# A PE-bound recurrent-attention and wave-mixing kernel: clock-keeping matmuls moved ahead of the spread of w, and a new order table

## The chip, the cores and the metric

The kernel runs on one core of one Trainium2 chip. The metric is the device time of one execution in microseconds (us), median of the runs. The engines are named as in the profile: PE (TensorE, matmuls), PEld (its weight loads), DVE (VectorE), ACT (ScalarE), POOL (GpSimd) and SP (SyncE, which only issues DMAs here).

## The reference

Two layers follow each other, for a batch of 4, 768 steps and 8 heads of 48:

```
for t in range(S):                       # one state of 48x48 per head
    cur   = outer(u * k_t, v_t)
    y_t   = r_t @ (state + cur)
    state = w * state + outer(k_t, v_t)
x   = heads of y side by side            # (4, 768, 384)
th  = x @ w_theta
yy  = w_tok_r @ (x * cos(th)) + w_tok_i @ (x * sin(th))   # over the 768 steps
u   = x + yy
out = u + max(u @ w_ch, 0)
```

## The kernel before

The recurrence is turned into matmuls over chunks of 128 steps. Powers of w that depend on the step are multiplied into r and k (`rscale` L553, `kscale` L566), the scaled tiles are transposed on PE (L516) and evacuated by ACT (L275), scores are formed (L614) and masked on DVE (L619), and the output of a pair of chunks is the sum of a masked part (L717) and a part from the running state (L712). The state is built from outer products (L672). The step's own term with u goes through `PD` (L626, L632), L641, `dg` and `yd` (L648, POOL). So one pair of chunks gives a piece of x (L726); there are three pairs in a batch element. From x come theta (L743), sine and cosine (L747, L750), `zr` (L753, DVE) and `zi` (L756, POOL). The token weights are loaded in row tiles 0 to 5 of each matrix, cast to bf16 on ACT or POOL, transposed on PE (L500) and evacuated; then the mixing (L774, 288 matmuls of 384 columns), `un` (L782), the channel matmul (L799), `fin` (L804) and the store (L808) follow. Mixing of one batch element is interleaved with attention of the next.

The tiles of the token weights in this text: `ld_99` to `ld_104` hold row tiles 0 to 2 (r0, i0, r1, i1, r2, i2), `ld_89` to `ld_94` tiles 3 to 5 (r3, i3, r4, i4, r5, i5). So `ld_90` is i3 and `ld_91` is r4.

The order of all work is written out by hand. `build` registers 816 tasks; the table `ORDER` (L27) lists each task's number, its engine (0 PE, 1 DVE, 2 ACT, 3 POOL, 4 SP) and the PSUM tiles that it takes, and `follow` (L178) emits them in that order. Each engine works through its own tasks strictly in that order and waits where an input is not there. The costs that stand with each task, such as `(1000, 217)`, are notes for the search that made the table; the emitted program does not use them.

The start matters here. The row w is loaded by ACT's queue (task 0, L336), spread over the 128 partitions by one f32 matmul against a row of ones (task 17, L405), and ACT takes its logarithm (task 18, L408) and six exponentials (tasks 19 to 24, L414) whose scale is the step number `tok_f` (POOL iota, task 8, then a DVE cast, task 9). These give the tables `wpow` for r, and `wpinvj` (first batch element) and `wpinv` for k.

Two groups of matmuls compute nothing. Both multiply a tile of zeros by itself into a PSUM tile that nobody reads: `before_w` (task 16, L402) and 108 `warm` tasks of two matmuls each (tasks 32 to 139, L817, depending on `zeros` and on the spread of w). The table scatters the warm tasks over places in PE's order; 28 of them (56 matmuls) stand behind the last useful matmul. They are called fillers below.

All loads go through SP's queue in table order, into a ring of 19 buffers.

Of the kernel before, what the change touches and what calls it, by code (L numbers as in the profile page):

```python
# [20 lines left out]
PE, DVE, ACT, POOL, SP = "PE", "DVE", "ACT", "POOL", "SP"  # L21
# [6 lines left out]
    (0, 2), (3, 1), (10, 3), (2, 1), (4, 1), (1, 2), (146, 4), (8, 3), (11, 1), (13, 3), (6, 1),  # L28
    (7, 2), (9, 1), (5, 1), (144, 4), (17, 0, 0), (14, 3), (153, 3), (145, 4), (16, 0, 1), (18,
    2), (12, 3), (24, 2), (20, 2), (15, 3), (178, 4), (19, 2), (32, 0, 4), (22, 2), (33, 0), (147,  # L30
    1), (34, 0), (21, 2), (35, 0), (25, 0, 2), (23, 2), (179, 4), (36, 0), (37, 0), (26, 1), (148,
    0, 1), (150, 1), (27, 2), (38, 0), (39, 0), (40, 0), (149, 2), (41, 0), (42, 0), (181, 1),
    (43, 0), (180, 4), (151, 0, 0), (44, 0), (164, 0, 3), (152, 2), (30, 1), (45, 0), (182, 0, 5),
    (184, 1), (142, 4), (46, 0), (28, 2), (47, 0), (154, 0, 1), (31, 3), (156, 0, 0), (160, 1),
    (212, 4), (155, 2), (48, 0), (49, 0), (50, 0), (157, 1), (51, 0), (187, 3), (52, 0), (161, 0,
    2), (165, 2), (53, 0), (158, 0, 1), (54, 0), (162, 2), (183, 2), (140, 4), (55, 0), (163, 3),
    (159, 1), (56, 0), (185, 0, 2), (168, 0, 0), (143, 2), (166, 0), (248, 4), (186, 2), (57, 0),
    (169, 0), (215, 3), (167, 1), (58, 0), (59, 0), (60, 0), (170, 1), (213, 4), (29, 2), (61, 0),
    (62, 0), (192, 0, 1), (198, 0, 2), (193, 1), (171, 0, 3), (249, 3), (199, 2), (270, 4), (63,
    0), (216, 0, 5), (172, 1), (141, 2), (64, 0), (188, 0, 0), (194, 1), (190, 0, 1), (214, 4),  # L40
    (189, 2), (200, 0), (218, 1), (65, 0), (66, 0), (217, 2), (67, 0), (68, 0), (191, 1), (69, 0),
    (195, 0, 3), (173, 0, 0), (269, 4), (196, 2), (197, 3), (201, 1), (70, 0), (202, 0, 1), (174,
    2), (268, 4), (71, 0), (203, 0), (175, 2), (72, 0), (221, 3), (219, 0, 2), (204, 1), (73, 0),
    (74, 0), (75, 0), (220, 2), (276, 3), (76, 0), (256, 4), (77, 0), (78, 0), (176, 1), (250, 0,
    3), (205, 0, 5), (251, 2), (79, 0), (224, 0, 1), (244, 4), (222, 0, 0), (225, 1), (273, 3),
    (80, 0), (232, 0, 2), (223, 2), (260, 4), (277, 0, 3), (206, 1), (233, 2), (81, 0), (226, 0,
    0), (264, 4), (278, 2), (82, 0), (228, 1), (274, 0, 5), (207, 0, 1), (227, 1), (245, 3), (275,
    2), (252, 4), (257, 3), (83, 0), (84, 0), (229, 0, 2), (208, 2), (284, 1), (306, 4), (85, 0),
    (282, 0, 0), (265, 3), (86, 0), (230, 2), (209, 2), (87, 0), (283, 1), (246, 0, 3), (272, 4),
    (88, 0), (231, 3), (285, 0, 2), (247, 2), (89, 0), (90, 0), (91, 0), (92, 0), (210, 1), (266,  # L50
    0, 5), (286, 2), (261, 2), (330, 4), (280, 0, 0), (258, 0, 3), (307, 3), (281, 1), (267, 2),
    (234, 0, 1), (235, 0), (177, 3), (253, 2), (308, 0, 2), (271, 4), (236, 1), (262, 0, 5), (259,
    2), (93, 0), (94, 0), (254, 0, 0), (332, 4), (95, 0), (211, 3), (263, 2), (237, 0, 1), (255,
    1), (96, 0), (97, 0), (396, 0, 3), (238, 1), (309, 2), (403, 0, 5), (310, 4), (239, 0, 0),
    (279, 2), (335, 3), (322, 4), (397, 0), (240, 2), (404, 0), (288, 0, 2), (398, 0), (241, 2),
    (302, 4), (289, 1), (287, 3), (405, 0), (292, 0, 1), (290, 0), (406, 0), (242, 1), (314, 4),
    (98, 0), (293, 0), (243, 3), (399, 0), (294, 1), (407, 0), (331, 4), (415, 0, 0), (416, 0),
    (291, 1), (417, 0), (303, 3), (336, 0, 1), (364, 4), (418, 0), (323, 3), (337, 2), (400, 0),
    (419, 0), (420, 0), (338, 3), (315, 2), (318, 4), (401, 0), (421, 1), (99, 0), (408, 0), (311,
    2), (402, 1), (304, 0, 2), (334, 4), (295, 0, 0), (409, 1), (305, 2), (324, 0, 1), (339, 0,  # L60
    3), (325, 1), (296, 2), (333, 4), (410, 0, 5), (319, 3), (340, 1), (316, 0, 2), (411, 2),
    (297, 0, 1), (317, 1), (369, 3), (365, 4), (346, 1), (312, 0, 5), (298, 2), (342, 0, 0), (366,
    4), (313, 1), (100, 0), (422, 0, 3), (299, 2), (343, 1), (341, 3), (423, 0), (424, 0), (326,
    4), (347, 0, 2), (350, 0, 5), (300, 1), (348, 2), (344, 0, 0), (349, 3), (351, 2), (320, 0,
    2), (486, 4), (345, 1), (425, 0), (321, 2), (352, 0), (426, 0), (372, 3), (354, 0, 1), (353,
    1), (328, 4), (427, 0), (355, 0), (428, 1), (441, 0, 5), (368, 4), (356, 1), (442, 0), (370,
    0, 0), (301, 3), (373, 0, 3), (367, 4), (371, 2), (434, 0, 2), (374, 1), (357, 0, 1), (443,
    0), (491, 3), (454, 4), (380, 1), (358, 2), (101, 0), (378, 0, 0), (102, 0), (329, 2), (103,
    0), (379, 1), (429, 0, 3), (455, 4), (327, 2), (444, 0), (359, 0, 1), (375, 2), (430, 1),
    (487, 4), (376, 0, 0), (360, 2), (435, 0), (377, 1), (436, 0), (453, 4), (361, 2), (445, 0),  # L70
    (461, 3), (381, 0, 3), (437, 0), (382, 2), (362, 1), (412, 0, 0), (457, 4), (383, 3), (492, 0,
    3), (413, 1), (438, 0), (493, 2), (456, 4), (439, 0), (446, 0), (440, 1), (384, 0, 0), (458,
    3), (431, 0, 1), (447, 1), (414, 4), (385, 1), (448, 0, 5), (488, 4), (432, 1), (386, 0, 0),
    (464, 3), (449, 2), (104, 0), (387, 0), (459, 0, 3), (490, 4), (388, 1), (462, 0, 2), (460,
    2), (105, 0), (106, 0), (473, 0, 5), (463, 1), (389, 0, 1), (489, 4), (494, 3), (450, 0, 0),
    (474, 1), (390, 2), (469, 1), (519, 4), (475, 0), (391, 0, 1), (476, 1), (363, 3), (451, 1),
    (495, 0, 2), (392, 2), (520, 4), (569, 0, 3), (496, 1), (570, 0), (393, 2), (550, 0, 5), (395,
    3), (502, 1), (571, 0), (521, 4), (497, 2), (551, 0), (394, 1), (552, 0), (572, 0), (606, 4),
    (467, 0, 0), (524, 3), (465, 0, 1), (468, 1), (503, 0, 2), (573, 0), (638, 4), (504, 2), (574,
    0), (506, 0, 2), (466, 1), (527, 3), (553, 0), (507, 2), (554, 0), (555, 0), (523, 4), (470,  # L80
    0, 0), (508, 0), (556, 1), (500, 0, 1), (471, 2), (575, 1), (498, 0, 0), (505, 3), (525, 0,
    5), (607, 4), (509, 1), (107, 0), (528, 0, 3), (501, 1), (526, 2), (557, 0, 2), (522, 4),
    (472, 3), (558, 0), (529, 2), (559, 0), (499, 1), (576, 0, 5), (605, 4), (560, 0), (643, 3),
    (477, 0, 1), (561, 0), (535, 1), (478, 0), (510, 0, 0), (530, 2), (479, 1), (433, 4), (511,
    0), (562, 0), (587, 0, 3), (512, 1), (480, 4), (577, 0), (610, 3), (108, 0), (531, 0, 1),
    (563, 1), (533, 0, 0), (109, 0), (532, 1), (588, 0), (513, 4), (536, 0, 2), (578, 0), (579,
    0), (534, 1), (539, 0, 1), (580, 0), (540, 2), (589, 0), (608, 4), (537, 1), (581, 0), (538,
    3), (541, 0, 0), (582, 1), (481, 0, 1), (639, 4), (613, 3), (110, 0), (542, 0), (482, 2),
    (609, 4), (590, 0), (543, 1), (594, 0, 2), (483, 2), (564, 0, 5), (595, 0), (485, 3), (565,
    2), (544, 4), (596, 0), (484, 1), (514, 0, 0), (566, 0, 1), (671, 4), (515, 2), (516, 2),  # L90
    (597, 0), (518, 3), (567, 1), (591, 0), (614, 0, 5), (640, 4), (517, 1), (598, 0), (611, 0,
    1), (616, 3), (599, 0), (615, 1), (452, 4), (612, 2), (592, 0), (545, 0, 0), (600, 1), (583,
    4), (593, 1), (621, 1), (619, 0, 1), (546, 2), (644, 0, 3), (620, 1), (622, 0, 2), (547, 2),
    (601, 4), (549, 3), (709, 0, 5), (710, 0), (623, 2), (711, 0), (645, 2), (548, 1), (625, 0,
    1), (702, 0, 2), (703, 0), (676, 3), (642, 4), (626, 1), (704, 0), (712, 0), (627, 0), (584,
    0, 0), (568, 4), (628, 1), (646, 3), (713, 0), (641, 4), (585, 1), (617, 0, 1), (677, 0, 3),
    (618, 1), (705, 0), (672, 4), (678, 2), (706, 0), (624, 3), (707, 0), (714, 0), (673, 4),
    (647, 0, 3), (715, 1), (629, 0, 0), (602, 0, 1), (648, 2), (708, 1), (675, 4), (649, 2), (727,
# [144 lines left out]
def build(ctx, tc, nc, r, k, v, w, u, moe_w_theta, moe_w_tok_r, moe_w_tok_i, moe_w_ch, out):  # L243
# [12 lines left out]
    P = Plan(SLOTS)  # L256
# [77 lines left out]
    def setup():  # L334
# [40 lines left out]
        def pads(ts):  # L375
            for t in ts:
                nc.gpsimd.memset(t[:, :, :, D:], 0.0)
        P.add({POOL: (750, 100)}, lambda e: pads(Rws), wr=[("Rw", i) for i in range(2)],
              prio=-197)
# [489 lines left out]
```

## Time and profile before

| what | value |
|---|---|
| median of 5 runs | 141.47 us (140.96 to 142.12) |
| the profiled execution's own time | 141.85 us |
| its span, first to last instruction | 140.2 us |
| PE busy | 134.6 us (96%), 1669 matmuls, 216 of them fillers of L817 |
| DVE, ACT, POOL busy | 102.6, 71.6, 89.2 us |
| last useful matmul group starts | 133.75 us, ends 134.90 us |
| DMA | 27.59 MB, mean 197 GB/s |

A matmul's duration in this profile is its latency, not its cost: matmuls overlap, and a group of n that the profile shows as taking t has a spacing of (t minus one latency) / (n - 1). The PE row counts fillers as busy, so "96%" is not a share of useful work.

### The profile page before, as it was taken

How to read it: one execution, taken by the hardware profiler on the slowest of the kernel's cores; microseconds unless marked ns; L12 is line 12 of the kernel's file. 1: busy time of each engine (PE TensorE's matmuls, PEld its weight loads, DVE VectorE, ACT ScalarE, POOL GpSimd, SP SyncE). 2: the span in 40 equal slices, each digit the busy share in tenths (PEclk: the TensorE clock that was granted, in tenths of full speed). 3: DMA queues.
4: the chain of work that ended last, by engine and by line, in shares of the span. 5: the costliest groups of instructions: out<-in, count | busy, mean ns of one | idle time of the engine just before them, and what ended most of it. 6: DMA issues, size and time to landing. Idle time of an engine off the chain costs nothing.

```text
span 140.2 us, 4016 instructions
## 1 busy us (share of the span) xinstructions
PE 134.6 (96%) x1669; PEld 98.1 (70%) x1669; DVE 102.6 (73%) x147; ACT 71.6 (51%) x110; POOL 89.2 (64%) x81
## 2 busy tenths in 40 slices
PE   3799999999999999999999999999999999999993
PEld 1698888788678778578667766766775756565673
DVE  5266897898375998789989965897799968344650
ACT  3845998899819747727625217671620044400020
POOL 7805838997998889694999769659384245400000
PEclk9999999999999999999999999999999999999999
DMA  3999999898999899969999687989499280907451
GB/s 101 269 261 294 311 202 293 277 317 163 310 308 232 188 289 178 207 151 214 188 218 208 177 154 142 208 213 259 99 250 174 56 98 19 281 2 188 148 180 50
DMA packets 72445, 27.59 MB, mean 197 GB/s; under 512 B 67050, under 2 KB 70891, under 8 KB 72427
## 3 DMA queue, kind: packets, MB, share of 16 engines
q1 hardware_dynamic: 72400, 27.34, 84.8%
q8 instruction: 13, 0.21, 0.7%
q14 instruction: 6, 0.04, 0.1%
q10 hardware_dynamic: 26, 0.00, 0.0%
HBM read 20.06 MB, written 4.72 MB: 177 GB/s over the span
## 4 chain that ended last, share of the span: by engine, by line
PE 86%; DMA 9%; ACT 1%; POOL 1%; DVE 0%; ACTq 0%; issue 0%; DVEq 0%
PE bank L774 34%; PE bank L516 10%; PE bank L799 8%; PE bank L817 8%; PE bank L743 8%; DMA ld<-in_moe_w_tok_i_dram 6%; PE bank L614 4%; PE bank L672 3%; PE bank L717 3%; DMA wu<-in_u_dram 3%; PE bank L712 2%; PE bank L500 2%; PE bank L641 1%; PE bank L680 1%; PE bank L600 1%; POOL ld L277 1%
## 5 line engine op out<-in xcount | busy, mean ns | idle before, releaser
L774 PE MATMUL bank<-zi,WiT 128*128 128x384 bf16 x144 | 33.5, 326 | 0.0
L774 PE MATMUL bank<-zr,WrT 128*128 128x384 bf16 x144 | 33.2, 326 | 0.0
L619 DVE TENSOR_TENSOR mAT<-bank,mask 128x1024 bf16<-128x1024 f32 x24 | 28.9, 1218 | 3.1 <-PE bank L614 2.8
L756 POOL TENSOR_TENSOR zi<-x,sin 128x768 bf16<-128x768 bf16 x12 | 19.6, 1640 | 10.9 <-ACT sin L747 10.9
L648 POOL TENSOR_TENSOR yd<-dg,vb 128x768 bf16<-128x768 f32 x12 | 17.6, 1472 | 8.0 <-ACT dg L275 6.7
L817 PE MATMUL bank<-zeros 128*128 128x128 bf16 x216 | 20.8, 232 | 0.0
L569 POOL TENSOR_TENSOR Kw<-ld,wpinv 128x768 bf16<-128x768 f32 x9 | 16.3, 1814 | 5.9 <-DMA ld<-in_k_dram 5.9
L275 ACT ACTIVATE RT<-bank 128x1024 bf16<-128x1024 bf16 x12 | 12.3, 1023 | 13.7 <-PE bank L516 12.6
L553 POOL TENSOR_TENSOR Rw<-ld,wpow 128x768 bf16<-128x768 f32 x10 | 18.1, 1815 | 1.0 <-DMA ld<-in_r_dram 1.0
L774 PEld LDWEIGHTS <-WrT 128*128 128x128 bf16 x144 | 12.8, 98 | 6.8
L774 PEld LDWEIGHTS <-WiT 128*128 128x128 bf16 x144 | 12.8, 97 | 6.7
L747 ACT ACTIVATE sin<-bank 128x768 bf16<-128x768 f32 x12 | 9.7, 810 | 15.1 <-PE bank L743 13.2
L804 DVE SCALAR_TENSOR_TENSOR fin<-bank,un 128x768 f32<-128x768 f32 (+1 forms) x13 | 11.5, 894 | 7.4 <-PE bank L799 7.3
L782 DVE TENSOR_TENSOR un<-bank,x 128x384 bf16<-128x384 f32 x24 | 12.7, 553 | 5.7 <-PE bank L774 5.1
L817 PEld LDWEIGHTS <-zeros 128*128 128x128 bf16 x216 | 14.7, 103 | 2.4 <-issue 0.3
L799 PE MATMUL bank<-Wch,uT 128*128 128x384 bf16 x72 | 13.7, 326 | 0.3 <-ACT uT L275 0.3
L743 PE MATMUL bank<-Wth,xT 128*128 128x384 bf16 x72 | 13.7, 326 | 0.0
L726 DVE TENSOR_TENSOR x<-bank,yd 128x768 bf16<-128x768 f32 x12 | 11.4, 956 | 3.1 <-PE bank L717 1.9
L753 DVE TENSOR_TENSOR zr<-bank,x 128x768 bf16<-128x768 f32 x12 | 11.4, 952 | 2.8 <-ACT bank L750 2.6
L750 ACT ACTIVATE bank<-bank,pi 128x768 f32<-128x768 f32 x12 | 10.5, 873 | 0.0
L275 ACT ACTIVATE uT<-bank 128x768 bf16<-128x768 bf16 (+1 forms) x5 | 3.3, 681 | 13.5 <-PE bank L516 13.5
L799 PEld LDWEIGHTS <-uT 128*128 128x128 bf16 x72 | 6.7, 98 | 4.5 <-ACT uT L275 0.5
(95 smaller groups left out, 221.1 us busy)
## 6 DMA issues: line engine op xcount, KB each, us to landing
ld<-in_r_dram SPq DMA_DIRECT2D x12, 384.0 KB, 5.6
out_dram<-fin SPq DMA_DIRECT2D x11, 384.0 KB, 2.6
ld<-in_k_dram SPq DMA_DIRECT2D x18, 192.0 KB, 4.4
ld<-in_v_dram SPq DMA_DIRECT2D x18, 192.0 KB, 5.5
ld<-in_moe_w_tok_i_dram SPq DMA_DIRECT2D x6, 384.0 KB, 6.1
ld<-in_moe_w_tok_r_dram SPq DMA_DIRECT2D x6, 384.0 KB, 5.6
ld<-in_v_dram SPq DMA_DIRECT2D x3, 384.0 KB, 6.0
ld<-in_k_dram SPq DMA_DIRECT2D x3, 384.0 KB, 6.2
```

The source lines that it names most:

```text
L275: nc.scalar.activation(dst, src, Act.Copy)
L516: nc.tensor.matmul(bank16(tok)[:, i * C:(i + 1) * C], s, ident, is_transpose=True, start=(i == 0), stop=(i == n - 1))
L553: P.add(mul(g, 2.15), lambda e: eng_of[e].tensor_mul(Rw[:, :, :, :D].transpose([0, 2, 1, 3]), Ls[ir].rearrange("p (h n d) -> p h n d", h=H ...
L569: eng_of[e].tensor_mul(Kw[:, :, :, :D].rearrange("p a h d -> p (a h) d"), Ls[ik].rearrange("p (a d) -> p a d", d=D), wpinv.rearrange("p a ...
L619: P.add({DVE: dve_op(8 * C)}, lambda e, tk=tk, c=c: nc.vector.tensor_mul(mAT[:, c].rearrange("p a h t -> p (a h) t"), dbl(tk).rearrange("p ...
L648: P.add({POOL: pool_op(2 * HD, 1.7)}, lambda e: eng_of[e].tensor_mul(yd.rearrange("p a (h d) -> p (a h) d", h=H), wide(dg, D), vb.rearrang ...
L743: nc.tensor.matmul(dbl(th)[:, t, :HD], xT[:, ND * t + dk, :], Wth[:, dk, :], start=(dk == 0), stop=(dk == ND - 1))
L756: P.add({POOL: pool_op(2 * HD, 1.9)}, lambda e: eng_of[e].tensor_mul(zi[:, 2 * pr:2 * pr + 2], x[:, 2 * pr:2 * pr + 2], sn), rd=xk + [("si ...
L774: nc.tensor.matmul(bank(tm)[:, :HD], WT[:, so, to * C:(to + 1) * C], z[:, so], start=(so == 0 and part == 0), stop=(part == 2 * NP - 1 and ...
L782: P.add({DVE: dve_op(HD)}, lambda e, tm=tm, t=t, to=to: nc.vector.tensor_add(un[:, t], bank(tm)[:, :HD], x[:, to]), use=[tm], rd=[("x", zj ...
L799: nc.tensor.matmul(dbl(tf)[:, t - lo, :HD], uT[:, ND * t + dk, :], Wch[:, dk, :], start=(dk == 0), stop=(dk == ND - 1))
L817: nc.tensor.matmul(bank("warm")[:, :C], zeros, zeros, start=True, stop=True, skip_group_check=True)
```

## The change

The values in the table change, and three notes on costs with it; one count in the code changes, from 8 to 9 matmuls in `before_w`. No other function differs.

```diff
-        P.add({ACT: (550, 1600)}, small_loads, wr=["w_row"], prio=-200)
+        P.add({ACT: (550, 950)}, small_loads, wr=["w_row"], prio=-200)
...
-        P.add({ACT: (1370, 3400)}, wu_load, rd=["table"], wr=["wu"], prio=-198)
+        P.add({ACT: (1370, 2800)}, wu_load, rd=["table"], wr=["wu"], prio=-198)
...
-            for _ in range(8):
+            for _ in range(9):
                 nc.tensor.matmul(bank("pre")[:, :C], zeros, zeros, start=True, stop=True,
                                  skip_group_check=True)
-        P.add({PE: (1000, 217)}, before_w, rd=["zeros"], acq=[("pre", 1)], prio=-201, name="pre")
+        P.add({PE: (510, 217)}, before_w, rd=["zeros"], acq=[("pre", 1)], prio=-201, name="pre")
...
 ORDER = [
-    (0, 2), (3, 1), (10, 3), (2, 1), (4, 1), (1, 2), (146, 4), (8, 3), (11, 1), (13, 3), (6, 1),
-    (7, 2), (9, 1), (5, 1), (144, 4), (17, 0, 0), (14, 3), (153, 3), (145, 4), (16, 0, 1), (18,
+    (0, 2), (4, 1), (10, 3), (3, 1), (2, 1), (16, 0, 0), (1, 2), (144, 4), (14, 3), (11, 1), (17,
+    0, 3), (7, 2), (13, 3), (145, 4), (32, 0, 4), (8, 3), (33, 0), (18, 2), (34, 0), (12, 3), (9,
...
```

On PE the order at the start was: L405, 8 of L402, 8 fillers, the small transpose L419 (it waits for the load of u), 4 fillers, transposes of r. It is now: 9 of L402, L405, 40 fillers, transposes of k, 4 fillers, L419, transposes of r, 10 fillers and so on. Of the 216 fillers of L817, 12 stood ahead of the first transposes and 56 behind the last useful matmul; now it is 40 and 58. In between there are 148 before and 118 after, and of these 118 all but 6 now stand ahead of the first mixing matmul.

On the other engines: `zeros` is the first instruction of DVE, not the third. POOL builds `spread` (task 14) and clears the pads of k's tiles (task 13) ahead of the iota (task 8). The six exponentials run in the order wpinv, wpinvj, wpow, wpinvj, wpinv, wpow, where it was wpinvj, wpow, wpow, wpinv, wpinv, wpinvj. DVE scales k before r. The cast of v for the first batch element (L277 on POOL, three times) is done by ACT; POOL casts one more token tile, and ACT six more of the half-state copies (L694) that DVE did as three instructions (L690). The third `rscale` moves from POOL to DVE and the third `kscale` from DVE to POOL.

On SP's queue the loads come as r, k, v, k, r, r, theta (2 of 3 parts), v, k, theta (1 of 3), then r and k of the second batch element, v, and six token tiles with r0 first; it was v, r, k, r, k, v, theta (1 of 3), r, theta (2 of 3), i0, k, and so on. The tile i3 (`ld_90`) was the 21st load and is the 22nd, with one more half load of v ahead of it. Its transposes on PE stand right behind the first two mixing matmuls.

## Prediction

> **What bounds the kernel now.** I read the page's head first, then PE's timeline of the first 22 us, then the chain, then busy time by stretch.
>
> ```profile
> span 140.2 us, 4016 instructions
> PE 134.6 (96%) x1669; PEld 98.1 (70%) x1669; DVE 102.6 (73%) x147; ACT 71.6 (51%) x110; POOL 89.2 (64%) x81
> PEclk9999999999999999999999999999999999999999
> L817 PE MATMUL bank<-zeros 128*128 128x128 bf16 x216 | 20.8, 232 | 0.0
> ```
>
> PE carries the span, but 216 of its matmuls are fillers, so its 96% must be split into needed work, fillers and stalls. The clock row shows nothing at the start; the spacing of equal matmuls does:
>
> ```profile
> 2.22 1.61 PE L405 MATMUL bank<-w_row,ones 1*128 1x384 f32 x2 [2.22 <-DMA w_row<-in_w_dram]
> 3.77 1.03 PE L402 MATMUL bank<-zeros 128*128 128x128 bf16 x8
> 4.59 1.06 PE L817 MATMUL bank<-zeros 128*128 128x128 bf16 x8
> 6.46 0.24 PE L419 MATMUL bank<-ident_f,wu 8*128 8x8 f32 x1 [0.80 <-DMA wu<-in_u_dram]
> ...
> 7.18 1.01 PE L516 MATMUL bank<-ident,Rw 128*128 128x128 bf16 x8
> 7.99 1.49 PE L817 MATMUL bank<-zeros 128*128 128x128 bf16 x12
> 9.27 1.06 PE L516 MATMUL bank<-ident,Kw 128*128 128x128 bf16 x8
> ...
> 11.41 0.86 PE L516 MATMUL bank<-ident,Rw 128*128 128x128 bf16 x8
> ...
> 13.08 0.73 PE L817 MATMUL bank<-zeros 128*128 128x128 bf16 x10
> ```
>
> Twelve fillers from 7.99: (1.49 - 0.31) / 11 = 107 ns apart. Ten from 13.08: (0.73 - 0.22) / 9 = 56 ns. The group at 11.41 is mixed. So PE ran at half speed until about 11.9 us, 5.4 us after its last gap (5.65 to 6.46, waiting for u).
>
> Needed work at full speed, spacing by the same arithmetic: mixing, theta and channel 432 matmuls x 162.5 ns = 70.2; transposes 258 + 72 at 56 = 18.3; scores 192 x 34 = 6.6; L717 192 x 25 = 4.8; L712 80 x 43 = 3.4; L672 40 x 55 + 60 x 44 = 4.8; L641, L680, L600 together 4.9. Sum 113.1 us. From the first transposes (7.2) to the end of the last channel matmul (134.9) are 127.7 us: 113.1 needed, 148 fillers x 56 ns = 8.2, cold surcharge on some 18 of these fillers 0.9 and on 32 needed matmuls 1.35, and 4.1 left over as stalls. Fillers and stalls lie almost all before 35 us: after it only about 34 fillers (1.9 us) and some 1.6 us of stalls stand between 94 us of needed work. The kernel is a ramp in which PE lacks input, then PE alone.
>
> What feeds the ramp: loads that land 1.5 us apart (DVE's timeline; the bracket is its wait).
>
> ```profile
> 7.60 0.96 DVE L566 TENSOR_TENSOR Kw<-ld,wpinvj 128x768 bf16<-128x768 f32 x1 [0.49 <-DMA ld<-in_k_dram]
> 9.04 0.96 DVE L553 TENSOR_TENSOR Rw<-ld,wpow 128x768 bf16<-128x768 f32 x1 [0.48 <-DMA ld<-in_r_dram]
> 10.54 0.96 DVE L566 TENSOR_TENSOR Kw<-ld,wpinvj 128x768 bf16<-128x768 f32 x1 [0.30 <-DMA ld<-in_k_dram]
> ```
>
> From 20 to 35 us (columns: length, then PE, PEld, DVE, ACT, POOL, clock, DMA share, GB/s) ACT is busy 13.99 of 15:
>
> ```profile
> 20.00:35.00 15.00, 14.91 (x274) 12.62 (x272) 12.85 (x15) 13.99 (x22) 12.47 (x11) 1.00 0.94 255
> ```
>
> And the chain (start, length, what) runs through a landing:
>
> ```profile
> 23.83 8.67 DMA ld<-in_moe_w_tok_i_dram
> 32.56 0.83 POOL ld L277
> 33.44 0.84 PE bank L500 x12
> ```
>
> This is tile i3: 8.7 us from issue, landed at 32.5, cast on POOL, transposed on PE at 33.44.
>
> **The change, part by part.**
>
> *Early fillers and clock.* `zeros` becomes DVE's first fill (0.88, 0.17 long), so L402 can start near 1.2; nine at 107 ns end at 2.2, when w lands. L405 starts as before (2.22) and ends at 3.83, so the logarithm is where it was (3.87): cost nothing, covered by the wait for w. Then 40 fillers, without a gap. When does the clock rise? By the nearest row, 5.4 us after the last gap: 1.2 + 5.4 = 6.6. The Trainium skill ("TensorE: Matmul & The Clock Gate", Part 1) states a window of about 3.4 us that runs freely: from 4.6, and up to 8.0 if a window had just begun. By 4.6 the 40 fillers end at 6.5, by 6.6 at 7.4 (26 cold, 14 warm), by 8.0 at 8.1. I take 6.6. The same section speaks against the change: it puts the ramp's penalty at under 1% of a typical span (1.4 us here). The rows say: 1.35 on needed work and 0.9 on fillers ahead of it, 2.25 us.
>
> *First inputs.* The iota now stands behind `spread` and k's pads on POOL (0.33 + 1.12 + 1.10), so `tok_f` comes near 4.4; the first exponential was at 4.38: at most 0.2 lost. With six exponentials 0.47 apart, both wpinvj stand after the fourth (6.4), k lands second (5.98): k scaled by 7.35, fillers done at 7.4, so transposes start at 7.4 against 7.2. r follows: scaled 8.25, ACT casts v (7.55 to 8.3), evacuates k (9.3) and r (10.4). Both together were ready at 11.4, but scores started only at 12.8, because PE was 1.5 us behind, in cold fillers. They now start near 10.4. On DVE behind it: masks from 12.0 (13.27), x of pair 0 near 15.7 (16.7), of pair 1 near 20.4 (23.2). First sine near 20.2 (22.2). So the front of the ramp moves by 2 to 2.8 us.
>
> *PE's sum.* 7.4 + 113.1 + 118 fillers x 56 ns = 6.6 + stalls. With stalls as before (4.1) the end is 131.2: 3.7 us earlier.
>
> *Do the later inputs follow?* ACT gets three casts of v (0.85 each) and the half copies. From the first to the third sine it worked 15.1 us almost without idle; I count 15.1 again, so the third comes near 35.3 (37.3): 2.0 gained, not more. DMA gains nothing from the clock: i3 has one half load more ahead of it. At the cadence without a pause it would land at 30.7; before it should by that have landed at 29.9 and landed at 32.5, the pauses in SP's queue being 2.6 us. Bounds 30.7 and 33.3. Its transposes stand as PE's third item of the mixing, and PE is in order: what waits behind are the first zi parts and all mixing; behind its cast on POOL wait zi of pair 1, `yd`, `rscale`. With landing at 33.3 PE passes there at 34.2, where it stood at 34.1 before with the same needed work done; with 30.7 it passes 2.3 earlier. I take the middle, 32.2: about 1.0 gained there. The next late tile, r4, comes out the same (0 to 1.5). Behind that point before had 1.9 us of fillers left, and after has 0.1 before the final group; of these 1.8 I take 1.1, as some covered real waits. Gain 1.0 + 1.1 = 2.1.
>
> *Free edits.* The 58 final fillers (56) lie beside the last evacuation and store. The half copies take ACT 0.66 where DVE took 0.56, three times, on an engine idle for half of the time after 50 us. L419 now behind k's transposes: u landed at 6.4, nothing waits for it on PE.
>
> **Rivals.**
> - *Likeliest: the ramp's inputs hold it to part of the gain*, 2.1 us: 141.5 - 2.1 = 139.4. Chance 0.45, own range 138.3 to 140.6.
> - *Full gain*: DMA pauses shrink, stalls stay 4.1: 3.7 us, 137.8. For it: the front moves 2 to 2.8 us, and fillers in the middle vanish. Against: ACT at 93% and the landings. 0.20.
> - *No change*: i3 lands at 33.3, r4 after 44, and the fillers that vanish turn into stalls of the same length, since each stood where an input was awaited: within 0.7 of 141.5, say 141.2. 0.15. Here belongs too that the clock rises only near 8.
> - *Slower*: place, the transposes of i3 in PE's order, in front of ready mixing. PE has 1.9 us in hand there (fillers dropped behind it), so the loss begins when it passes after 36.0, that is when i3 lands after 35.1, 1.8 later than my late bound. Each us beyond is one us of the span. A pause of SP's queue like the 2.6 us before, once more, on top: 33.3 + 2.6 = 35.9, and the same again at r4 (0.6): 1.4 lost, 142.9. 0.20.
>
> **Numbers.** The sums are against the profiled execution (span 140.2; 141.85 with what lies around it), 0.4 above the median; I apply the difference to the median: 139.4. Faster by over 0.5% (0.7 us, about what a measurement of this kernel can tell from no change) 0.65, within 0.15, slower 0.20. Range 137.2 to 142.2: it takes in the full gain and leaves out half of the slower case.
>
> **What would show it.** Twelve of the early fillers near 6 us at 107 then 56 ns shows the clock step; scores at 10.4 the front; third sine at 35.3 ACT; landing of i3 and the wait of L500 behind the first L774 show the DMA limit. Mixing spaced at 162 ns without idle from 45 to 133 us shows that the dropped fillers were not needed. Wrong if the clock rises after 8, if i3 lands after 35, or if new idle appears on PE after 45 us, say behind DVE, busy 14.06 of 15 us from 65 to 80.

## The result, and the profile after

The changed kernel takes 141.45 us (median of 44 executions, 140.72 to 142.33) against 141.81 of the kernel before, measured beside it (79 executions). The ratio is 0.998, 95% interval 0.9967 to 0.9993. The forecast was 2.1 us; 0.36 came. A ratio in this text leaves out executions more than 1.5% above the fastest of their kernel, a median does not. Each profile is of one execution.

The page's head and its row of fillers, after:

```profile
span 139.8 us, 4021 instructions
PE 135.3 (97%) x1670; PEld 97.3 (70%) x1670; DVE 100.5 (72%) x144; ACT 76.3 (55%) x119; POOL 85.5 (61%) x78
L817 PE MATMUL bank<-zeros 128*128 128x128 bf16 x216 | 19.1, 237 | 0.0
```

PE is as full as before, and that again says little. Its timeline of the start:

```profile
1.05 1.14 PE L402 MATMUL bank<-zeros 128*128 128x128 bf16 x9 [1.05 <-DVE zeros L350]
2.21 1.61 PE L405 MATMUL bank<-w_row,ones 1*128 1x384 f32 x2
3.75 4.45 PE L817 MATMUL bank<-zeros 128*128 128x128 bf16 x40
8.06 0.86 PE L516 MATMUL bank<-ident,Kw 128*128 128x128 bf16 x8
...
9.69 0.72 PE L817 MATMUL bank<-zeros 128*128 128x128 bf16 x10
```

The 40 fillers are (4.45 - 0.31) / 39 = 106 ns apart, so all of them ran at half speed. The ten at 9.69 are (0.72 - 0.22) / 9 = 56 ns apart. Single records put the step at 8.6 us, inside the transposes of k. Before it was at 11.9.

DVE's timeline shows two things that held the front back:

```profile
4.20 0.64 DVE L369 CAST tok_f<-tok_i 128x6 f32<-128x6 int32 x1 [2.50 <-POOL tok_i L366]
...
6.96 0.96 DVE L566 TENSOR_TENSOR Kw<-ld,wpinvj 128x768 bf16<-128x768 f32 x1 [1.33 <-ACT wpinvj L414]
...
11.63 1.58 DVE L553 TENSOR_TENSOR Rw<-ld,wpow 128x768 bf16<-128x768 f32 x1
13.14 2.50 DVE L619 TENSOR_TENSOR mAT<-bank,mask 128x1024 bf16<-128x1024 f32 x2
```

The cast of the step numbers holds the first exponential until 4.93 (before 4.38; I took 4.6 at most), and `rscale` of the next chunks stands right ahead of the masks. It took 1.58 us here, against 0.95 for the other instructions of its kind. The masks start at 13.14; before it was 13.27.

From 20 to 35 us (length, then busy time of PE, PEld, DVE, ACT, POOL, then clock, DMA share, GB/s) ACT and DVE are a little fuller than before, 14.12 and 13.22 of 15 (13.99 and 12.85):

```profile
20.00:35.00 15.00, 15.00 (x261) 12.17 (x260) 13.22 (x17) 14.12 (x21) 12.80 (x11) 1.00 1.02 303
```

To follow a gain through the run I add up the needed matmuls by the spacings listed in the prediction (113.5 us in all) and read from the trace when so much of it was done. All times in us:

| needed work done | before | after | e5 | e6 | e7 | e2 | e17 |
|---|---|---|---|---|---|---|---|
| 3 | 12.77 | 13.36 | 11.24 | 14.62 | 13.11 | 13.19 | 13.04 |
| 18 (about the first mixing) | 35.01 | 34.52 | 33.88 | 36.70 | 33.93 | 34.35 | 33.68 |
| 40 | 58.48 | 57.61 | 57.35 | 59.80 | 57.02 | 57.44 | 56.78 |
| 90 | 110.60 | 109.04 | 109.58 | 111.23 | 108.45 | 108.87 | 108.21 |
| 98 | 118.54 | 117.65 | 117.53 | 119.28 | 116.51 | 116.93 | 116.26 |
| last useful matmul ends | 134.90 | 134.01 | 133.89 | 135.64 | 132.87 | 133.29 | 132.63 |
| span ends | 140.15 | 139.75 | 137.93 | 139.77 | 137.01 | 139.25 | 136.37 |

Between before and after: 0.59 lost at 3 us of work (there the work comes in bursts, and with slightly other spacings the sign turns), 0.49 gained at 18, 1.56 at 90. Then it falls to 0.89 at 98, and to 0.40 at the end of the span. Two losses behind 110 us took more than half of what the change had earned. The chain of the changed kernel names the first:

```profile
108.71 0.98 PE bank L774 x6
111.11 4.20 DMA uT<-un
115.36 1.15 PE bank L799 x6
...
134.01 3.24 PE bank L817 x58
```

A transposition by DMA took 4.20 us from issue to landing, and PE waited for it. In the kernel before, the four from 104.9 to 128.1 of which a landing is recorded took 2.73 to 3.93 us, and PE did not wait for one. The second loss is behind the last useful matmul: 5.74 us to the end of the span, 5.25 before.

### The profile page after: what moved, and what is told of

It reads as the page before. It is cut to its first block, busy times and chain, and to the rows that moved or that the text cites. A ratio compares the mean times of both kernels' runs of the same rounds, so it can differ in the third digit from the quotient of the medians.

```text
span 139.8 us, 4021 instructions
## 1 busy us (share of the span) xinstructions
PE 135.3 (97%) x1670; PEld 97.3 (70%) x1670; DVE 100.5 (72%) x144; ACT 76.3 (55%) x119; POOL 85.5 (61%) x78
## 4 chain that ended last, share of the span: by engine, by line
PE 90%; DMA 3%; DVE 2%; ACT 2%; issue 1%; DVEq 0%
PE bank L774 33%; PE bank L516 10%; PE bank L817 9%; PE bank L799 8%; PE bank L743 7%; PE bank L614 5%; PE bank L717 4%; PE bank L672 3%; DMA uT<-un 3%; PE bank L500 3%; PE bank L712 3%; PE bank L641 1%; PE bank L405 1%; DVE Rw L553 1%; PE bank L680 1%; PE bank L402 1%
## 5 line engine op out<-in xcount | busy, mean ns | idle before, releaser
L774 PE MATMUL bank<-zr,WrT 128*128 128x384 bf16 x144 | 33.4, 326 | 0.0
L817 PE MATMUL bank<-zeros 128*128 128x128 bf16 x216 | 19.1, 237 | 0.0
L569 POOL TENSOR_TENSOR Kw<-ld,wpinv 128x768 bf16<-128x768 f32 x9 | 16.3, 1814 | 2.5 <-DMA ld<-in_k_dram 2.5
L553 POOL TENSOR_TENSOR Rw<-ld,wpow 128x768 bf16<-128x768 f32 x9 | 16.3, 1815 | 1.4 <-PE bank L743 1.4
L817 PEld LDWEIGHTS <-zeros 128*128 128x128 bf16 x216 | 14.8, 107 | 2.9 <-issue 2.0
L774 PEld LDWEIGHTS <-WrT 128*128 128x128 bf16 x144 | 12.1, 97 | 6.3
L799 PE MATMUL bank<-Wch,uT 128*128 128x384 bf16 x72 | 13.7, 327 | 0.6 <-DMA uT<-un 0.4
L799 PEld LDWEIGHTS <-uT 128*128 128x128 bf16 x72 | 6.8, 98 | 5.4 <-DMA uT<-un 0.8
L750 ACT ACTIVATE bank<-bank,pi 128x768 f32<-128x768 f32 x12 | 10.5, 876 | 0.0
```

Source lines behind the costliest of these rows:

```text
L553: P.add(mul(g, 2.15), lambda e: eng_of[e].tensor_mul(Rw[:, :, :, :D].transpose([0, 2, 1, 3]), Ls[ir].rearrange("p (h n d) -> p h n d", h=H ...
L569: eng_of[e].tensor_mul(Kw[:, :, :, :D].rearrange("p a h d -> p (a h) d"), Ls[ik].rearrange("p (a d) -> p a d", d=D), wpinv.rearrange("p a ...
L774: nc.tensor.matmul(bank(tm)[:, :HD], WT[:, so, to * C:(to + 1) * C], z[:, so], start=(so == 0 and part == 0), stop=(part == 2 * NP - 1 and ...
L799: nc.tensor.matmul(dbl(tf)[:, t - lo, :HD], uT[:, ND * t + dk, :], Wch[:, dk, :], start=(dk == 0), stop=(dk == ND - 1))
L817: nc.tensor.matmul(bank("warm")[:, :C], zeros, zeros, start=True, stop=True, skip_group_check=True)
```

## The experiments

Theory T (the prediction's): the clock rises early, other engines and the landings hold the ramp to a part of it. Rivals: F, the fillers in PE's fixed order hold back the work behind them; D, DVE's rscale or the late step numbers hold the front. Later came theory I, on PE's instruction fetches. Each ratio is to the kernel before on the same chip, with its 95% interval.

**e1.** Old table, early `zeros`, nine L402 ahead:

```diff
+move(4, 3)
+move(16, 17)
-            for _ in range(8):
+            for _ in range(9):
```

> The old table with the clock part alone: zeros filled first, 9 zero matmuls ahead of the spread of w, 17 more fillers over the wait for u, so that PE never pauses. The clock should rise near 8.6 us as in the changed kernel (11.9 before). Theory 'other engines and loads hold the ramp': PE's scores come about 1 us earlier, but the first mixing matmul moves by under 0.4 us and the total by under 0.3. Rival 'the clock is worth its cold surcharge': 1.5 us or more less than before (ratio 0.99 or lower). Rival 'fillers hold PE': no gain, since all fillers of the ramp are still there.

As built it did not get the further fillers over the wait for u that the text speaks of (the edit read the loop variable after the loop had ended). 142.32 us, ratio 1.0034 (1.0001 to 1.0067). The gap for u stayed and the clock rose at 12.2. Nine matmuls at 1 us, by themselves, bring nothing.

**e2.** Changed kernel without L402 (its 40 fillers stayed in, other than the text says):

```diff
-            for _ in range(9):
+            for _ in range(0):
```

> The new table without the 9 zero matmuls and without the 40 fillers ahead of the first transposes: PE idle from 3.8 to 7.9 us, clock late (near 12 us or later). Theory 'other engines and loads hold the ramp': within 0.5 us of the changed kernel. Rival 'the early clock is what the new table lives from': 1.5 to 3 us more, as 30 fillers and some 60 needed matmuls of the stage from 8 to 12 us cost 50 ns more each.

140.67 us, ratio 0.9922 (0.9894 to 0.9950): faster than the changed kernel (141.30 in e3, timed beside it), by leaving out nine matmuls that nobody waits for. The clock rose at 8.3 all the same. By the table it stays within 0.2 us of the changed kernel up to 90 us of work, and then it does not have the wait for `uT`. This was the first hint of what follows.

**e3.** As built this was the changed kernel itself, so it is a repeat.

> The new table without the 112 fillers between the first transposes and the first mixing matmuls (6.2 us of PE time at full clock). Rival 'fillers hold PE': PE's queue moves up wherever an input is there, first mixing 1 us earlier or more, total 1 to 2 us less. Theory 'other engines and loads hold the ramp': the fillers' time turns into waiting, first mixing within 0.4 us, total within 0.4 us, if the clock stays up; if the clock falls in the gaps it shows as 107 ns spacing, and the total is longer.

141.30 us, ratio 0.9973 (0.9951 to 0.9995). Clock at 8.8, and the wait for `uT` again: both belong to the program.

**e4.** The third rscale back on POOL:

```diff
-(215, 1)
+(215, 3)
```

> The new table with the third scaling of r (task 215) back on POOL, where it was before the change; POOL idles there from 14.65 to 17.5 us. DVE has 0.95 us less between the first masks and x. Theory 'DVE's queue is what took the front's gain': x of pair 0 starts near 16.3 (17.19), theta and the first sine 0.5 to 0.9 earlier, total 0.3 to 0.8 less. Rival 'fillers hold PE': x 0.9 earlier but theta unmoved within 0.3, total within 0.2.

141.38 us, ratio 0.9959 (0.9939 to 0.9978). Needed work lies 0.25 us earlier than in the changed kernel from its third microsecond on (the clock rose at 7.6 in this execution), and is level at 18. Theory D in this form falls.

**e5.** Old table, gapless start: e1 and 17 more fillers ahead of L419.

```diff
-                for _ in range(2):
+                for _ in range(19 if i == 3 else 2):
```

> The old table with the clock part alone, now with the 17 more fillers really in place over the wait for u (in e1 and e3 the loop variable stood at its last value when the fillers were emitted, so these edits of single fillers had not taken). Clock near 8.5 us instead of 11.9. Theory 'other engines and loads hold the ramp': scores 1 us earlier, first mixing within 0.4 us, total within 0.3 us of before. Rival 'the clock is worth its cold surcharge': ratio 0.99 or lower.

140.79 us, ratio 0.9937 (0.9915 to 0.9959). Start of PE:

```profile
3.78 2.85 PE L826 MATMUL bank<-zeros 128*128 128x128 bf16 x25
6.58 0.21 PE L428 MATMUL bank<-ident_f,wu 8*128 8x8 f32 x1
6.72 0.40 PE L826 MATMUL bank<-zeros 128*128 128x128 bf16 x4
7.16 0.61 PE L525 MATMUL bank<-ident,Rw 128*128 128x128 bf16 x8
```

The four at 6.72 are (0.40 - 0.22) / 3 = 60 ns apart: full speed before the first needed transposes, at 6.6. On the old table the early clock alone is worth 1.1 us at 18 us of work and 1.0 at the last useful matmul. The profile is of the fastest execution, 139.63, and the end of its span follows sooner, too (below); between the medians it is 0.9.

**e6.** Changed kernel with a late clock: no fillers ahead of the first transposes, and no L402 (`range(0)`).

```diff
-                for _ in range(2):
+                for _ in range(0 if i < 20 else 2):
```

> The new table without the 9 zero matmuls and without the 40 fillers, now really taken out: PE idle from 3.8 to 7.9 us, clock late. Theory 'other engines and loads hold the ramp': within 0.5 us of the changed kernel (141.4). Rival 'the early clock is what the new table lives from': 1.5 to 3 us more.

142.03 us, ratio 1.0030 (1.0005 to 1.0054). Full speed only from about 12.4; 2.2 us later than the changed kernel at 18 us of work, 1.6 at the last useful matmul. With a late clock the new table is slower than the old one with its late clock, by 0.74 us at the last useful matmul. The early fillers do their work.

**e7.** Changed kernel without the 112 fillers between first transposes and mixing:

```diff
-                for _ in range(2):
+                for _ in range(0 if 20 <= i < 76 else 2):
```

> The new table without the 112 fillers between the first transposes and the first mixing (6.2 us of PE time at full clock). Rival 'fillers hold PE': first mixing 1 us earlier or more, total 1 to 2 us less. Theory 'other engines and loads hold the ramp': the fillers' time turns into waiting, first mixing and total within 0.4 us, if the clock stays up; if the clock falls in the gaps, 107 ns spacing and a longer total.

139.23 us (138.72 to 141.06), ratio 0.9832 (0.9791 to 0.9873). So theory F looked right. But the table gives F at most 0.59 us at 18 us of work: 112 x 56 ns = 6.3 us of fillers went, and nine tenths of that came back as waits. Against e18 below, whose clock rose at 7.3 as here and not at 8.6, it is 0.34 us. In the stretches from 12 to 24 us, in the columns named above:

```profile
12.00:18.00 6.00, 4.89 (x78) 4.35 (x80) 5.94 (x7) 4.32 (x7) 2.74 (x3) 0.72 1.20 272
18.00:24.00 6.00, 5.33 (x85) 3.76 (x79) 4.32 (x6) 5.30 (x8) 5.50 (x4) 1.00 0.95 257
```

PE pauses, and for that the clock was granted at 0.72 in the first stretch (half speed from 14.1 to 17.5). DVE, at 5.94 of 6, is what is full. The rest of the gain had to come from elsewhere.

**e8.** No L402 and no fillers at all ahead of the middle (`0 if i < 76 else 2`).

> The new table without any of the zero matmuls ahead of the mixing (only the 64 at its end and middle stay): the clock depends on the needed matmuls alone. Theory 'other engines and loads hold the ramp': clock near or after 20 us, PE's needed work of the ramp takes twice as long but still fits between its waits: total 0 to 1.5 us above the changed kernel. Rival 'the clock is worth its surcharge': 3 us or more above. If it is faster than the changed kernel, the fillers cost more than the clock gives.

143.0 us (140.77 to 144.99), ratio 1.0028 (0.9991 to 1.0065) of its seven fastest. Its profile is of a long execution (144.63): matmuls of 128 columns stand 107 ns apart up to 25.9 us. Without fillers the early clock is gone and with it the gain.

**e9.** e5 without the old table's ramp fillers (`0 if 6 <= i < 79`).

> The old order table with the gapless start (nine matmuls first, then fillers without a pause over the wait for u), and in addition without the fillers that the old table has between the first transposes of k and the last channel matmul. Theory F (fillers in PE's fixed order delay the needed work behind them, whichever table they stand in): faster than the same kernel with its fillers (140.8 before, last useful matmul at 133.9) by about as much as the new table gained, 1.1 us at the last useful matmul and 1 to 2 us in the time, so 139 to 139.8. Theory T (the new table put its fillers in front of ready work, the old one only where PE had to wait anyway): the last useful matmul stays within 0.3 us of 133.9, the time near 140.8. If the clock falls in the gaps: above 141.

140.88 us, ratio 0.9918 (0.9892 to 0.9944). At 18 us of work it stood at 33.98, beside e5's 33.88 and e7's 33.93: e5, e7, e9 and e13 all come to the same floor, so early clock and missing fillers do not add up in the ramp. Theory T holds for it, with a reservation: without its fillers e9's clock fell to half speed from 10.1 to 16.9. Behind the ramp it gained on e5: its last useful matmul ends at 133.13 (forecast by T within 0.3 of 133.9), 0.26 after e7's, and yet the time is 1.65 us above e7's.

**e10.** Half of the ramp fillers (`1 if 20 <= i < 76 else 2`).

> The changed kernel with one matmul instead of two in each of the 56 ramp filler tasks, so 56 fillers are gone. Theory F: the time is between that with all of them (141.4) and that with none (139.2), near 140.3, and the last useful matmul ends near 133.4. If the clock is what counts and falls in the kernel with none, half of them keeps it up and the time is at or below 139.2. If only waits were filled, no change from 141.4.

138.97 us (138.78 to 139.89), ratio 0.9808 (0.9772 to 0.9845). The clock stays up (granted 1.00 from 12 to 30 us). Its profile is of the slowest execution and ends the last useful matmul at 134.04, as the changed kernel does, yet took 139.89 and not 141.47. In this execution 18 us of work were done only at 35.1 (the clock had risen at 9.0), so what it gained came behind the last useful matmul.

**e11.** e7, and the iota first on POOL (`move(8, 14)`).

> The changed kernel without its ramp fillers, and with the iota for the step numbers as POOL's first work again, ahead of the spread and of k's pads. The step numbers should be cast by 3.9 us instead of 4.9 and the first exponential start at 4.4. Theory D (the late start of the six exponentials and so of the scaled k is what holds the front): first transposes at 7.5 instead of 8.1, everything up to the first mixing 0.4 to 0.6 us earlier, time 138.6 to 138.9. Theory F alone (after the fillers the next limit is elsewhere, in the landings or DVE): within 0.2 us of 139.2.

Executions at 138.61 and 138.98, and four between 142.63 and 143.18; the ratio of 0.9792 (0.9733 to 0.9852) rests on the first two. In the profile (138.98) the first exponential starts at 4.45, the first transposes at 7.76, and 18 us of work are done at 33.42, 0.5 earlier than in e7. Theory D is right about the step numbers at the first transposes. The 0.5 is not theirs alone: in e7 the clock fell in the ramp, here it stayed at 1.00. At 70 us of work nothing is left of it (87.75 against 87.78). The four long executions had a mean granted clock of 0.952 to 0.964, the two short ones 1.0: long times without fillers go with a fallen clock.

**e13.** The kernel before without its ramp fillers (`0 if 6 <= i < 79`).

> The kernel before without its fillers between the first transposes of k and the last channel matmul, its start untouched, with the wait for u still there. Theory F without regard to the clock: about 1 us faster than before, 140.6. Theory C (the fillers do keep the clock, so that without them and with a start that has a gap PE stays at half speed through more of the ramp): clock up after 13 us, needed work late by 1 us or more at 13 us, and the time 141.5 to 143. It tells how much of the gain without fillers needs the early clock.

141.63 us (139.97 to 142.24), ratio 0.9953 (0.9925 to 0.9981). 18 us of work at 33.80: on the old table, too, some fillers did hold work back, even with the clock rising only near 13. Of the 1.2 us gained there 0.9 were left at the last useful matmul.

**A new theory.** In every trace the rows of the DMA queues have a queue of instructions:

```profile
q8 instruction: 13, 0.21, 0.7%
```

These are blocks of 16,384 bytes. From the second on they are 122 to 128 matmuls apart on average, whichever kernel, so they follow PE's progress and not the time: PE's program is being fetched. The Trainium skill ("Runtime: NRT & Kernel Launch", Instruction fetch mechanics) says that an engine's instruction memory is refilled in blocks of 256 instructions by a DMA of its own, and that this is mostly hidden. The count agrees (3,340 matmuls and weight loads / 13 = 257), and no row shows PE waiting for one. But others wait. Where the last fetch falls, and how long the end takes from the last useful matmul to the end of the span:

| kernel | last fetch begins | last useful matmul ends | to the end of the span |
|---|---|---|---|
| before | 135.8 | 134.90 | 5.25 |
| after | 134.2 | 134.01 | 5.74 |
| e1, e2, e3, e4 | 135.0, 133.7, 135.7, 135.0 | 134.78, 133.29, 134.70, 134.14 | 6.05, 5.95, 5.58, 5.27 |
| e8, e9, e13 | 138.9, 134.1, 135.2 | 136.89, 133.13, 133.99 | 6.03, 5.38, 5.86 |
| e5, e7, e11 | 130.8, 131.8, 131.8 | 133.89, 132.87, 133.13 | 4.04, 4.14, 4.13 |
| e6 | 141.5 (behind the span) | 135.64 | 4.13 |
| e10 | 122.7 | 134.04 | 4.15 |

A fetch within 2 us behind the last useful matmul, where the last two stores run, goes with 5.25 to 6.05 us; none there, with 4.04 to 4.15, and all these kernels have the fillers at the end. And `uT`: in the changed kernel, e3, e4, e16 and e18, where a fetch begins 1.8 to 2.0 us after the issue near 111 us, the transposition takes 4.17 to 4.34 us, and PE stands 0.5 to 0.7 us in front of L799; in e2, e6, e8, e10, e14 and e17, without one, 2.76 to 2.77, and PE does not stand there. In between lie e7 and e11, where the fetch begins about with the issue (3.35 and 3.73). The old table has one near 104 us: 3.84 to 4.03 us in the kernel before, e1 and e9, with a fetch 0.3 to 0.6 us after the issue, and 3.09 to 3.30 in e5, e19 and e13, without; in e15 it took 4.68 with a fetch 2.1 us after the issue. A fetch is not the only thing that lengthens a transposition: the one issued near 86 us takes 4.22 us in the changed kernel with no fetch in it. The transposition's part of the DMA page, first the changed kernel, then e2 (111 to 115.5 us), the last column being the us from issue to landing:

```profile
q8 instruction: 1, 0.02, 1.5%
...
uT<-un SPq DMA_TRANSPOSE x1, 4.2
```

```profile
uT<-un SPq DMA_TRANSPOSE x2, 2.8
```

Four more kernels, and then two, put the theory to the test.

**e14.** e2 without the 62 fillers from just ahead of the last channel matmul on (`0 if i >= 77 else 2`). No useful instruction moves.

> The changed kernel without the nine first matmuls (as in e2) and without the 58 fillers behind the last useful matmul and the 4 just ahead of it. Theory I (a fetch of PE's instructions that falls into the last store holds that store for 1.5 to 2 us): the program ends before the 13th fetch, the last store lands 2.0 us after its issue, and the time is 139.0, 1.6 below e2's 140.7, though no useful work is moved. Rival (the store's landing varies by itself, and fillers behind the last useful matmul cost nothing): the time is that of e2, 140.7, and the store takes 3.4 to 4.2 us.

138.92 us, ratio 0.9827 (0.9790 to 0.9865). Its needed work is within 0.1 us of e2's all along; the end of the span follows 3.72 us behind the last useful matmul and not 5.95. Theory I forecast 139.0, its rival 140.7.

**e15.** The kernel before without its 58 last fillers and the 8 of L402.

> The kernel before without its 58 fillers from the last channel matmul on and without the 8 matmuls of L402, its clock start left late. Theory I: 13th fetch gone, last store 2.0 us, time 139.9, 1.6 below the kernel before, with the last useful matmul still ending near 134.9. Rival: within 0.5 us of the kernel before.

140.10 us, ratio 0.9892 (0.9853 to 0.9931), with the end of the span 3.71 us behind the last useful matmul (5.25 before). That matmul ended at 134.06 and not near 134.9 as forecast; in this execution, one of the two fastest, the clock rose at 10.5 and not at 11.9.

**e16.** e7 without L402, to move the fetch back into the stores.

> The kernel e7 (the changed kernel without its ramp fillers, 139.2 us) and in addition without the nine first matmuls, which shifts the 12th fetch of instructions from 131.8, ahead of the last stores, to about 133.1, into them. Theory I: last store 3.4 to 4.2 us, and the time rises by 1.5 us to about 140.8, although nine matmuls less are computed and the last useful one ends as before, near 133. Rival: 139.2.

143.55 us (140.31 to 145.03), ratio 0.9963 (0.9918 to 1.0007) of its five fastest. The fetch came at 135.4, close ahead of the last stores; the last but one took 3.00 us and not 2.09, the span ended 4.80 us behind the last useful matmul (e7: 4.14), and a fetch at 114.6 made `uT` take 4.17. But most of the time has another cause. The clock was at half speed from 14.8 to 25.1, and the last useful matmul ended at 135.60:

```profile
18.00:24.00 6.00, 5.89 (x44) 3.32 (x41) 3.59 (x5) 3.54 (x6) 4.79 (x4) 0.50 0.88 243
```

The 0.50 is the granted clock; PE gets 44 matmuls done where e7 gets 85. So the size of this time says nothing on fetches. It says that without fillers in the ramp the clock can stay down for 10 us. Three executions had a mean granted clock of 1.0; they took 140.31, 140.47 and 140.78 us, near the 140.8 of theory I, but none of them was profiled.

**e17.** Half of the ramp fillers, iota first, none at the end.

> What the runs point to together: the changed kernel with one matmul in each ramp filler task, the iota first on POOL, and no fillers behind the last useful matmul. Last useful matmul near 133.0, last store 2.0 us, nothing of PE behind it: 138.3 us, below 139.0 of the kernel with half the ramp fillers. If the iota does nothing for a kernel that has fillers, 138.8.

138.59 us (138.10 to 138.94), ratio 0.9791 (0.9756 to 0.9826): the fastest that was run, 2.9 us below the changed kernel's median. (Its column in the table is of its fastest execution.)

**e18.** The changed kernel with one edit, `0 if i >= 77 else 2`: 1608 matmuls, no 13th fetch.

> The changed kernel with one edit: the 58 fillers behind the last useful matmul and the 4 just ahead of it are left out. Theory I: the last matmul is number 1608, and the 13th fetch came near number 1611 to 1633 in the other programs, so it should not come. The 12th still comes near 113 us and holds the transposition (4.2 us). Last useful matmul near 134.0, 3.7 us from there to the end of the span, time 139.5, against 141.4 of the changed kernel. Rival: 141.4.

139.83 us, ratio 0.9862 (0.9811 to 0.9913). The last useful matmul ends at 134.00 (134.01 in the changed kernel), the span 2.0 us earlier (in its fastest execution; 1.6 between the medians). DMA from 133 to 139 us in 40 slices, the kernel before, the changed kernel and then this one:

```profile
DMA  4000000000001899999999999972000000000000
GB/s 154 0 0 0 0 0 0 0 0 0 0 0 72 307 420 369 328 379 447 359 338 348 369 318 399 358 266 72 10 20 21 31 20 31 20 31 20 0 0 0
...
q8 instruction: 1, 0.02, 1.0%
```

```profile
DMA  0000001999899999930000000899710000000000
GB/s 0 0 0 0 0 0 72 396 369 389 317 338 348 369 338 389 338 123 10 10 10 10 10 20 31 317 389 338 277 31 20 31 20 31 10 0 0 0 0 0
...
q8 instruction: 1, 0.02, 1.8%
```

```profile
DMA  0000001999999999999991000000000000000000
GB/s 0 0 0 0 0 0 72 328 410 369 338 389 369 379 338 358 410 369 338 358 359 62 0 0 0 0 0 0 0 0 0 0 0 0 0 0 0 0 0 0
```

The last two show the same 560 packets of store. In the changed kernel the stream breaks off at 135.6 us, trickles for a microsecond, comes again at 136.7 and has a thin end until 138.2; in e18 it runs through in 2.3 us. The kernel before has such a thin end, too. In trickle and thin end the packets come nearly one at a time, at 10 to 31 GB/s against some 350.

Not all of the 2.0 us is the fetch. With all fillers at the end and no fetch in the stores (e5, e6, e7, e10, e11) the span ends 4.04 to 4.15 us behind the last useful matmul, which is 0.9 us behind the last filler; without these fillers (e14, e15, e17, e18, e19) it ends after 3.71 to 3.75, which is 1.6 us behind the landing of a store. Estimate from these: of e18's 2.0 us about 1.6 go with the fetch and 0.4 with the fillers themselves.

**e19.** Old table, gapless start, half of its ramp fillers, none at the end.

> The old table with the gapless start (as in e5), one matmul instead of two in each of its ramp filler tasks, and none behind the last channel matmul. If the new table is worth something of itself: 139.1 or more, as e5's and e9's last useful matmul ended at 133.9 and 133.1, against 132.6 and 138.6 for the new table in e17. If the tables are equal once the fetch and the fillers are out of the way: 138.6.

139.26 us, ratio 0.9805 (0.9755 to 0.9855). By the bar set above, 139.1 or more, that speaks for the new table, and the last useful matmul ends at 134.17 against 132.63 in e17. But the interval covers e17's, e17 has the iota first besides, and in the two profiles the clock rose at 9.9 here and at 8.0 in e17. So with half the fillers and no fetch in the stores the new table is not told apart from the old one.

## Why the prediction was wrong

**The clock.** Step: "By the nearest row, 5.4 us after the last gap: 1.2 + 5.4 = 6.6." In the profiled execution it rose at 8.6, outside the bounds of 4.6 to 8.0. Other executions that start alike on PE rose at 6.6 and 6.7 (e5, e9), 7.3 to 8.0 (e7, e18, e11, e4, e17), 8.8 and 9.0 (e3, e10) and 9.9 (e19), those without L402 at 7.0, 8.0 and 8.3 (e14, e16, e2). So L402 makes no difference that shows, and the moment is a matter of the execution, over some 3.3 us. That is what a window running freely would do, as the Trainium skill has it ("TensorE: Matmul & The Clock Gate", Part 1), and its 3.4 us agree with the runs: the stretches of half speed in the ramp of e7, e9 and e16 last 3.41, 6.83 and 10.24 us, one, two and three times 3.41 (length, busy times, then the clock as 0.50):

```profile
14.12:17.53 3.41, 3.41 (x48) 3.07 (x47) 3.37 (x4) 3.14 (x4) 0.52 (x2) 0.50 1.22 279
10.11:16.93 6.82, 6.25 (x80) 4.93 (x80) 5.50 (x8) 5.20 (x10) 5.42 (x5) 0.50 1.17 308
14.83:25.06 10.23, 9.82 (x106) 7.03 (x104) 6.76 (x9) 7.45 (x11) 7.58 (x5) 0.50 0.99 265
```

Estimate: with one such window to two, rises from 6.6 to 9.9 begin to count near 3.1 us, while L405 runs, and not at 1.2 as the prediction had it. My value was the early end of such a spread taken for the middle, and the 5.4 us of the kernel before, from which it came, was a single draw. What that cost can be read from e18, the same program up to the last channel matmul, whose clock rose at 7.3: its scores come at 11.21, 0.25 us ahead of the changed kernel's, and at 18 us of work it is still 0.25 ahead.

**The front.** Step: "the front of the ramp moves by 2 to 2.8 us". First transposes 8.06 (7.4 forecast), scores 11.46 (10.4), masks 13.14 (12.0), x of pair 0 17.19 (15.7, before 16.7), of pair 1 23.57 (20.4, before 23.2), third sine 38.23 (35.3, before 37.3; ACT took 16.3 us from the first sine, not the 15.1 counted). Parts of this that the trace shows: the late cast of the step numbers, and the rscale ahead of the masks. k was scaled at 7.92 (7.35 forecast), and e18, with its fillers done by 7.8, had to wait for that and began its transposes at 8.06 all the same. e11 takes away the first part: transposes 0.3 us earlier. Of the 1.06 us that the scores came late, 0.25 is the clock (e18), 0.4 the fillers ahead of them (e18 to e7, 11.21 to 10.79) and 0.2 the step numbers (e7 to e11, 10.59). e4 moved another rscale than the one at 11.63, so that one's share is argued.

**The ramp.** Step: "about 1.0 gained there", at i3. It was 0.49 (35.01 to 34.52 at 18 us of work). i3 itself was no limit: its cast on POOL ran at 33.03 and PE took up its transposes at 34.02 without a wait. Theory T is right that the ramp has a floor other than PE: with and without fillers, old table or new, e5, e7, e9, e11, e13, e17 and e19 come to between 33.4 and 34.0. The changed kernel stops at 34.5, 0.6 above e7; of these 0.25 go with its late clock (e18), 0.34 with fillers. What sets the floor itself was not tried. So this term was mis-sized by half.

**Behind the ramp.** Step: "of these 1.8 I take 1.1". Between 18 and 90 us of work the gain grew from 0.49 to 1.56, by 1.07. This term was right in size. That it came from the dropped fillers is argued: taking the old table's fillers out brought 0.9 us there in e9 (against e5) and nothing in e13 (against before). (In the sum of needed work, 330 transposes at 56 ns are 18.5 us and not 18.3; nothing hangs on it.)

**The step that failed.** The largest part of the missing gain lies behind 90 us of work, in what the prediction put at nothing: "The kernel is a ramp in which PE lacks input, then PE alone", and "The 58 final fillers (56) lie beside the last evacuation and store", at no cost. By 90 us of work 1.56 of the forecast 2.1 us was there. Then 0.67 went up to 98 us of work, 0.55 of it to a slow `uT`, and 0.49 more at the end of the span (which with a fetch in the stores varies by itself from 5.25 to 6.05 us). Both are DMAs that the useful work waits for, and both hold a fetch of PE's instructions. The last fillers are not free: they carry the program over the boundary of its 13th block, and that fetch lies in the last stores, before and after alike. e18 takes them out alone: 1.6 us between the medians, 2.0 in the span, of which some 0.4 is the fillers' own length. As before had this loss as well, it is a gain that was to be had and not what the change lost, and the 0.49 is no more than that variation. What the change did was move the fetches: the 12th began at 114.3 in the kernel before, between two transpositions of `uT`, and at 113.0 in the changed one, inside `uT`. e2 took nine matmuls away at the start, the same fetch came at 116.2, behind `uT`, and 1.61 us of gain were there at the last useful matmul. For `uT` this rests on the runs that agree, above all on e2, which leaves out nothing that is waited for; no run moves the fetch and nothing else, so it is well supported and not isolated.

The rival "no change" gave 141.2, near the time, by luck: its reason (i3 late, fillers turned into stalls of the same length) is not what happened behind the ramp. Within the ramp e7 shows the second half of it to be nine tenths true. That "the clock rises only near 8", which I had put with it, was about right, and cost 0.25 us. The rival "slower" was wrong in its place: i3. My own warnings, a clock that rises after 8 and new idle on PE after 45 us, both came true, the second in front of L799 at 115 us, and not behind DVE.

Left open: what in the fetch holds the store's packets (they come nearly one at a time, so one late strand would do), which queue or engine they share, and whether the fetches at 13.8, 18.1 and 28.7 us delay loads in the ramp as well. This was not tried.

## What to carry to other kernels

A matmul that computes nothing still costs instructions. Count them, find the rows of instruction fetches among the DMA queues, and see whether one of them falls into a store or a transposition that somebody waits for; moving or dropping some fillers can be worth more than what they were put in for. Fillers against a falling clock belong where PE would wait anyway, and half as many were enough here: judge by when a given amount of needed work is done, and by the end behind the last useful matmul, each by itself.

## What was not expected of the hardware

- A transposition of 2.76 us with a fetch of 16,384 bytes 1.8 to 2.0 us behind its issue took 4.17 to 4.34, and with a fetch in the last stores the span ended 5.25 to 6.05 us behind the last useful matmul, against 4.04 to 4.15 with the same fillers and no fetch there.
- The clock's rise lay between 6.6 and 9.9 us for starts that are the same on PE, with nine matmuls more or less at 1 us.
- With pauses of PE in the ramp the clock fell to half speed for 3.41 us (e7), 6.83 (e9) or 10.24 (e16), multiples of one length; one matmul in place of two in each filler task kept it at 1.0 in all seven executions of e10.
- The same rscale instruction took 1.58 us on DVE at 11.6 us, with POOL's L440 at work beside it for 0.77 us, and 0.95 at 15.55. In e13 a kscale took 0.96 with 0.61 us of L440 beside it, so when this costs is open.
